# First batch's q and k loaded in rows of eight tokens and transposed by TensorE, and w1 and w2 in chunks of another shape

## The chip, the cores and the metric

The kernel runs on one core of a Trainium2 chip. It is one launch. The time is device microseconds of that core, and the number that is compared is the median of the runs. The engines are TensorE (PE in the profile, its weight loads PEld), VectorE (DVE), ScalarE (ACT), GpSimd (POOL) and SyncE (SP), which issues the DMA transfers. Each engine works through its own instructions strictly in order.

## The reference, cut to what matters

```
B, H, S, D = 8, 8, 576, 64;  pool = 8
k_p = k.reshape(B, H, 72, 8, D).mean(axis=3)          # v_p likewise
scores = q @ k_p.T / sqrt(D)                          # 576 x 72 for each of 64 heads
attn = exp(scores - max);  attn = attn / (attn.sum + 1e-09)
x = (attn @ v_p), heads side by side                  # 4608 tokens x 512
a = x @ w1;  b = x @ w2                               # 512 -> 1024
x = ((a * b) @ w3) @ w_out                            # 1024 -> 1024 -> 512
h = x @ w_in;  g = h / (1 + exp(-1.702 h));  out = g @ w_out2   # 512 -> 2048 -> 512
```

q, k and v are float32, the weights are float64.

## The kernel before

All large products run as three matmuls of values that are split into a rounded part and a remainder (`split`, `mm3`). The float64 weights come in as pairs of 32-bit words and are turned into float32 on the chip. There are three stages.

*The start-up.* `Conv.step` converts one chunk of 128x512 weights in each call: ACT writes two pieces (L166, L167), DVE shifts (L168) and merges (L171), GpSimd adds (L174). The intermediate e lies either in one of two PSUM banks (`acc` in the profile) or in the SBUF tile `cv`. A later call splits the result (L104). A chunk of w3 is transposed on TensorE between (L476). w3 times w_out is multiplied out to one matrix wp (L113 to L115, into `acc`), a product for each chunk that is ready; two rows of wp are open at a time.

Beside it runs the attention of batch 0. A *pair* is two heads of one batch; pairs 0 to 3 are batch 0. A pair passes through steps that `tick` calls in turn: g0 (k and q into the layout that the scores need, sums of k over eight tokens), g1 (scores, L271; their maximum, L276; the subtraction, L278), g2 (exp), g3 (normalize, L292 to L295), g4 (transposed weights), g6 (times v; writes x, L382 and L383). For pairs 0 to 3, g4 lets TensorE transpose; later pairs are transposed by DVE in g3 (L306, tile p). In g0, `g_load` has fetched k and q as four blocks each, with a head's 32 of 64 columns in 32 partitions (`load_blocks`, L228). DVE transposes them in 32x32 blocks (L254 for k, L255 for q) and sums k over eight tokens (L257). ACT puts the sums into the block-diagonal kbd (L259, L260), which is the moving operand of the scores.

*The main loop.* Nine blocks of 512 tokens, eight f each: x·w1 and x·w2 into the banks wk0 and wk1, the product a·b on DVE (L612), and the product of the step before with wp into `acc`. Two ticks of the attention run in each f, so later pairs are computed beside it. The weights w1 and w2 are kept in tiles that are freed in the last block. Some of the freed tiles serve as landing places for the first loads of the next stage: four x tiles (L602) and one of w_in (L606). Which f they start at is set by `FA`.

*The second MoE* (from L692 on).

What sets the order: the calls in the loop over `conv.step` and `tick` give the program order, and a scheduler then sets the order of the instructions on each engine before the run. All DMA transfers stand in one order on SP. An SP issue waits for the eighth issue before it to land, and for its buffer to be free. `take` and `give` hand out the slots (tiles of 128x1024 words), in which chunks, w3 tiles and x lie; a slot is free for the next load when all its readers are done.

## Time and profile before

| | us |
|---|---|
| runs | 1561.65, 1558.10, 1560.19 |
| median | 1560.19 |
| profiled execution | 1560.06 |
| its span | 1558.3 |
| TensorE busy in the span | 1498.2 (96%) |
| DVE busy | 982.5 (63%) |
| ACT busy | 618.4 (40%) |
| GpSimd busy | 586.3 (38%) |
| mean granted clock | 0.974 |

The profiled execution is 1.76 us longer than its span.

How the rows below are read. A row of the table by stretches gives a stretch, its length and then for each engine the busy time and, in brackets, the instructions; PEclk is the granted clock of TensorE as a share of 2.4 GHz; the DMA share is that of the core's 16 DMA engines. A row of the timeline gives the start, the time to the end of the last of the instructions it groups, engine, line, operation, output and input tile, form and count, and in square brackets the idle time before it and what ended it. A row of the grouped instructions gives the form, count, busy time in us and mean ns of one, and after the bar the idle time before them and its releasers. Tile names stand without their numbers there. SPq is the queue of SP; what counts there is the time of issue. A float32 matmul of unsplit values, as L271's, shows two records for each call.

### The profile page before, as it was taken

The page shows a single profiled execution, that of the slowest core. Times are in us where ns is not written, and L with a number is a line of the kernel's source. Part 1 is how long each engine was busy: PE and PEld are TensorE (multiplying, and loading weights), DVE is VectorE, ACT ScalarE, POOL GpSimd, SP SyncE. Part 2 cuts the span into 40 slices and gives each one's busy share as a digit, 9 for nine tenths or more (in the row PEclk, how much of TensorE's full clock was granted, in tenths as well). Part 3 has the DMA queues.
Part 4 walks back from the last instruction along what each step waited for, and adds up shares of the span by engine and source line. Part 5 has one row for each costly group of instructions (what it writes and reads, how often), then busy time and mean ns, then how long its engine had stood idle before and what let it go on. Part 6 is the DMA issues. An engine that isn't in the chain of part 4 may idle for free.

```text
span 1558.3 us, 19571 instructions
## 1 busy us (share of the span) xinstructions
PE 1498.2 (96%) x6728; PEld 1235.8 (79%) x6728; DVE 982.5 (63%) x1810; ACT 618.4 (40%) x1202; POOL 586.3 (38%) x660
## 2 busy tenths in 40 slices
PE   5866999999999999999989999999999999999998
PEld 4744888888888888887868888888888888888887
DVE  8899888787787877569563334463446254734441
ACT  7774443433443434366643323242234222422331
POOL 7688555555555545369462211100110011101110
PEclk9965999999999999999989999999999999999999
DMA  9962223323232320189769343423343233423310
GB/s 289 242 162 53 54 53 67 68 59 68 52 73 47 77 43 35 42 309 371 303 211 391 107 149 115 132 92 117 126 130 114 101 115 122 149 69 127 125 52 28
DMA packets 225444, 196.33 MB, mean 126 GB/s; under 512 B 158784, under 2 KB 175168, under 8 KB 225344
## 3 DMA queue, kind: packets, MB, share of 16 engines
q1 hardware_dynamic: 224768, 194.03, 41.1%
q8 instruction: 53, 0.87, 0.2%
q10 hardware_dynamic: 576, 1.05, 0.2%
q14 instruction: 47, 0.39, 0.1%
HBM read 150.99 MB, written 44.04 MB: 125 GB/s over the span
## 4 chain that ended last, share of the span: by engine, by line
PE 85%; DVE 6%; DMA 3%; issue 2%; ACT 2%; SPq 1%; POOL 0%; DVEq 0%; ACTq 0%; POOLq 0%
PE bk L692 22%; PE bk L113 8%; PE bk L115 8%; PE bk L114 8%; PE wk L114 8%; PE wk L115 8%; PE wk L113 8%; PE acc L113 4%; PE acc L114 4%; PE acc L115 4%; PE wk L271 2%; DMA s<-in_moe_w_dram 2%; DVE cv L171 1%; SPq L228 1%; DVE s L104 1%
## 5 line engine op out<-in xcount | busy, mean ns | idle before, releaser
L692 PE MATMUL bk<-xM,st 128*128 128x512 f32 x1080 | 261.4, 389 | 0.0
L113 PE MATMUL wk<-s,s 128*128 128x512 f32 x576 | 230.9, 403 | 8.8 <-DVE s L104 4.4
L692 PEld LDWEIGHTS bk<-xM,st 128*128 128x128 f32 x1080 | 202.6, 188 | 42.5 <-ACT o L709 0.4
L114 PE MATMUL wk<-s,s 128*128 128x512 f32 x576 | 228.6, 397 | 6.9 <-DVE s L383 6.9
L115 PE MATMUL wk<-s,s 128*128 128x512 f32 x576 | 228.1, 397 | 0.0
L113 PE MATMUL bk<-wo,mv 128*128 128x512 f32 x576 | 224.1, 389 | 0.1
L114 PE MATMUL bk<-wo,mv 128*128 128x512 f32 x576 | 224.1, 389 | 0.0
L115 PE MATMUL bk<-wo,mv 128*128 128x512 f32 x576 | 210.0, 389 | 0.0
L306 DVE STREAM_TRANSPOSE p<-s_t 32x160 f32<-32x160 f32 (+1 forms) x560 | 178.5, 319 | 11.0
L828 POOL TENSOR_TENSOR s<-s,sg 128x512 f32<-128x512 f32 x32 | 41.4, 1292 | 333.2 <-ACT sg L827 333.2
L113 PE MATMUL acc<-s,s 128*128 128x512 f32 x352 | 134.6, 404 | 8.6 <-ACT s L103 8.1
L104 POOL TENSOR_TENSOR s<-a,s 128x512 fp32r<-128x512 f32 x56 | 72.4, 1294 | 186.4 <-ACT s L103 145.9
L114 PE MATMUL acc<-s,s 128*128 128x512 f32 x352 | 141.3, 401 | 0.3 <-POOL s L104 0.3
L115 PE MATMUL acc<-s,s 128*128 128x512 f32 x352 | 140.8, 400 | 0.3 <-DVE s L104 0.3
L113 PEld LDWEIGHTS wk<-s,s 128*128 128x128 f32 x576 | 110.2, 192 | 33.7 <-DVE s L104 6.0
L114 PEld LDWEIGHTS wk<-s,s 128*128 128x128 f32 x576 | 110.5, 192 | 30.6 <-DVE s L383 8.3
L115 PEld LDWEIGHTS wk<-s,s 128*128 128x128 f32 x576 | 110.4, 192 | 23.4
L113 PEld LDWEIGHTS bk<-wo,mv 128*128 128x128 f32 x576 | 108.1, 188 | 23.0 <-ACT mv L103 0.5
L115 PEld LDWEIGHTS bk<-wo,mv 128*128 128x128 f32 x576 | 108.1, 188 | 22.5
L114 PEld LDWEIGHTS bk<-wo,mv 128*128 128x128 f32 x576 | 108.1, 188 | 22.4
L174 POOL TENSOR_TENSOR cv<-cv,s 128x512 int32<-128x512 int32 x72 | 99.7, 1389 | 56.2 <-DVE cv L171 23.9
L844 DVE TENSOR_TENSOR q<-bk,m 128x512 f32<-128x512 f32 x32 | 22.1, 692 | 150.7 <-PE bk L692 150.7
(155 smaller groups left out, 2546.1 us busy)
## 6 DMA issues: line engine op xcount, KB each, us to landing
st<-wind SPq DMA_DIRECT2D x89, 512.0 KB, 3.7
s<-in_moe_w_dram SPq DMA_DIRECT2D x32, 512.0 KB, 6.4
wind<-s SPq DMA_DIRECT2D x32, 512.0 KB, 5.7
s<-in_moe_w_out_dram SPq DMA_DIRECT2D x24, 512.0 KB, 6.6
s<-wind SPq DMA_DIRECT2D x23, 512.0 KB, 3.7
kr<-in_k_dram SPq DMA_DIRECT2D x128, 72.0 KB, 2.5
qr<-in_q_dram SPq DMA_DIRECT2D x128, 72.0 KB, 2.5
out_dram<-o SPq DMA_DIRECT2D x36, 256.0 KB, 2.0
```

The source lines that it names most:

```text
L104: lo_eng.tensor_tensor(out=dst[:, 1], in0=src, in1=f32(dst[:, 0]), op=ALU.subtract)
L113: nc.tensor.matmul(o, a[:, 0, a_sl], b[:, 0, b_sl], start=first, stop=False)
L114: nc.tensor.matmul(o, a[:, 0, a_sl], b[:, 1, b_sl], start=False, stop=False)
L115: nc.tensor.matmul(o, a[:, 1, a_sl], b[:, 0, b_sl], start=False, stop=last)
L171: nc.vector.scalar_tensor_tensor(out=wu, in0=hi_w, scalar=0x80000000, in1=eu, op0=ALU.bitwise_and, op1=ALU.bitwise_or)
L174: nc.gpsimd.tensor_tensor(out=w.bitcast(I32), in0=w.bitcast(I32), in1=lo_w.bitcast(I32), op=ALU.add)
L228: nc.sync.dma_start(dst[32 * c:32 * c + 32], src[b, 2 * hp + c // 2, :, 32 * (c % 2):32 * (c % 2) + 32].rearrange("(g t) d -> t g d", t=32))
L271: nc.tensor.matmul(sc[half][:, i * KW:(i + 1) * KW], qT[:, sl(tt)], mov, start=True, stop=True)
L306: nc.vector.transpose(out=dst[:, :nt, 32 * c:32 * c + 32], in_=s_t[32 * c:32 * c + 32, :nt, 32 * r:32 * r + 32])
L692: nc.tensor.matmul(o, w[:, x, m], b[:, y], start=first and n == 0, stop=last and n == 2, skip_group_check=True)
L828: eng.tensor_tensor(out=v, in0=v, in1=sg, op=ALU.mult)
L844: nc.vector.tensor_tensor(out=q_, in0=o, in1=m1, op=ALU.add)
```

## The change

For the four pairs of batch 0 (`n < NS`), q and k are loaded in rows of eight tokens: a partition holds eight consecutive tokens of a head, 512 numbers, so that 72 partitions hold a head, and one DMA (L242) fetches the two heads of a pair. The tiles come from the slots. `g0_first` takes the place of g0's DVE work. TensorE multiplies pieces of 72x64 with the identity: for k, 16 calls, which accumulate the eight tokens of a row into columns 288 to 359 of the bank wk2, so that the sum over eight tokens comes out of the product (L267); for q, 8 calls for each half of the tokens into wk2 and wk3 (L275). DVE copies the first half into qT and ACT the second (L278).

`g_load` is called two pairs ahead instead of one, pairs 0 and 1 are loaded before most of the weights (depth 2, then 9), ticks start at the third step instead of the fifth, and the loop has two steps more. The chunks of w1 and w2 are 256 rows of w by 256 columns, instead of 512 by 128, and the loop over f picks its half of such a tile; w1's lower parts of the split go to GpSimd and w2's to DVE as before. `FA` is 3 instead of 2, and the tiles are given back two f at a time. In the new file the lines stand lower: L168 is L169, L171 is L172, L254 is L288, L271 is L305, L306 is L340, L383 is L417, L612 is L654, L692 is L734.

```diff
@@ -54,6 +54,7 @@
     NB = NT // T
     NG = B * HP
     NPE = HP
+    NS = HP
     SB = S // 32
     TT = (S + P - 1) // P
     KW = 2 * SK
@@ -148,7 +149,7 @@
                 t = take((P, T, 2), U32)
                 d = t.rearrange("p n two -> p (n two)")
                 nc.sync.dma_start(
-                    d if len(src.shape) == 2 else d.rearrange("p (c m) -> p c m", c=KM), src)
+                    d if len(src.shape) == 2 else d.rearrange("p (c m) -> p c m", c=src.shape[1]), src)
                 self.staged.append((t, turn, done))
 
         def step(self):
@@ -234,6 +235,13 @@
             if n >= NG:
                 return
             b, hp = divmod(n, HP)
+            if n < NS:
+
+                for g, src in ((g_k, k), (g_q, q)):
+                    g[n] = take(dtype=F32)
+                    nc.sync.dma_start(
+                        g[n][:SK], src[b, 2 * hp:2 * hp + 2].rearrange("h (s u) d -> s h (u d)", u=POOL))
+                return
             g_k[n] = pa.tile([P, S], F32, name="kr", tag="raw", bufs=4).rearrange("p (g d) -> p g d", d=32)
             load_blocks(g_k[n], k, b, hp)
             g_q[n] = pa.tile([P, S], F32, name="qr", tag="raw", bufs=4).rearrange("p (g d) -> p g d", d=32)
@@ -248,7 +256,33 @@
             nc.sync.dma_start(g_v[n], vr[:P])
             nc.sync.dma_start(vtr[:KT], vr[P:])
 
+        def g0_first(n):
+
+            kn, qn = g_k.pop(n), g_q.pop(n)
+            ps = wk[2:]
+            w = POOL // 2 * SK
+            kp = ps[0][:, w:w + SK]
+            for a in range(2):
+                for u in range(POOL):
+                    nc.tensor.matmul(kp[sl(a, D)], kn[:SK, a, sl(u, D)], ident[:SK, :SK],
+                                     start=u == 0, stop=u == POOL - 1)
+            nc.scalar.copy(kbd[:D, 0], kp[:D])
+            nc.scalar.copy(kbd[D:, 1], kp[D:])
+            qv = qT[:, :S].rearrange("p (s u) -> p u s", u=POOL)
+            for h, eng in ((0, nc.vector.tensor_copy), (1, nc.scalar.copy)):
+                for i in range(POOL // 2):
+                    for a in range(2):
+                        nc.tensor.matmul(
+                            ps[h][sl(a, D), sl(i, SK)], qn[:SK, a, sl(POOL // 2 * h + i, D)],
+                            ident[:SK, :SK], start=True, stop=True)
+                eng(qv[:, POOL // 2 * h:POOL // 2 * (h + 1)],
+                    ps[h][:, :w].rearrange("p (u s) -> p u s", s=SK))
+            give(kn, qn)
+            g_load(n + 2)
+
         def g0(n):
+            if n < NS:
+                return g0_first(n)
             kr, qr = g_k.pop(n), g_q.pop(n)
             kT = pa.tile([P, S], F32, name="kT", tag="kT")
             nc.vector.transpose(out=kT, in_=kr.rearrange("p g d -> p (g d)"))
@@ -258,7 +292,7 @@
                 out=ks, in_=kT.rearrange("p (s u) -> p s u", u=POOL), op=ALU.add, axis=AX.X)
             nc.scalar.copy(kbd[:D, 0], ks[:D])
             nc.scalar.copy(kbd[D:, 1], ks[D:])
-            g_load(n + 1)
+            g_load(n + 2)
 
         def g1(n):
             sc = (wk[2], wk[3])
@@ -505,7 +539,7 @@
                         w = wp_s[it] = take()
                         split(w, acc[it % 2], nc.vector)
 
-        FA = 2
+        FA = 3
         n_mm, seen, seen_o = {}, [], []
 
 
@@ -524,24 +558,31 @@
         for it in range(2, NIT):
             for jh in range(2):
                 add_3(it, jh)
-        for f in range(NF1):
-            conv.add(col_tile(w1, f), None,
-                     conv.to(w1_s, f, a=f - FA if 0 <= f - FA < NA else None))
-            conv.add(col_tile(w2, f), None, conv.to(w2_s, f, nc.vector))
-
+
+        slots_a = list(range(NA))
+        for h in range(NF1 // 2):
+            for w, w_s, eng in ((w1, w1_s, nc.gpsimd), (w2, w2_s, nc.vector)):
+                for c in range(KM // 2):
+                    conv.add(w[sl(c, 2 * P), sl(h, 4 * P)].rearrange("(c p) m -> p c m", p=P), None,
+                             conv.to(w_s, (c, h), eng, a=slots_a.pop(0) if h and slots_a else None))
+
+        conv.depth = 2
         conv.load()
         g_load(0)
         v_load(0)
+        g_load(1)
+        conv.depth = 9
+        conv.load()
         conv.ps = acc[2:]
         n3 = 8 + 2 * NIT
         done3 = []
-        for i in range(n3 + 4):
+        for i in range(n3 + 6):
             key = conv.step()
             if done3:
                 w3_mm(done3.pop(0))
             if key is not None:
                 done3.append(key)
-            if i >= 4 and tick_n[0] < 20:
+            if i >= 2 and tick_n[0] < 20:
                 tick()
         conv.depth = 8
         give(*(wo_s.pop(j) for j in list(wo_s)))
@@ -590,12 +631,13 @@
                 if conv.busy():
                     conv.step()
                 pa_, pb_ = wk[0], wk[1]
-                for ps, w in ((pa_, w1_s[f]), (pb_, w2_s[f])):
+                h, j = divmod(f, 2)
+                for ps, w_s in ((pa_, w1_s), (pb_, w2_s)):
                     for c in range(KM):
-                        mm3(ps, w, sl(c), x[c], slice(0, T), c == 0, c == KM - 1)
+                        mm3(ps, w_s[c // 2, h], sl(c % 2 * 2 + j), x[c], slice(0, T), c == 0, c == KM - 1)
                 if blk == NB - 1:
-                    give(w1_s.pop(f))
-                    give(w2_s.pop(f))
+                    if j:
+                        give(*(w_s.pop((c, h)) for w_s in (w1_s, w2_s) for c in range(KM // 2)))
                     if 0 <= f - FA < KM:
 
                         t = take_a(f - FA)
```

The first place is DVE's order around pair 0's q and k. Before:

```order
L171 SCALAR_TENSOR_TENSOR cv_310<-s12_142,acc3_69 128x512
L104 TENSOR_TENSOR s2_266<-cv_201,s2_266 128x512
L168 TENSOR_SCALAR acc2_68<-acc2_68 128x512
L254 STREAM_TRANSPOSE kT_219<-kr_146 128x576
L104 TENSOR_TENSOR s4_348<-cv_260,s4_348 128x512
L171 SCALAR_TENSOR_TENSOR cv_338<-s13_144,acc2_68 128x512
L255 STREAM_TRANSPOSE qT_114<-qr_151 128x576
L257 TENSOR_REDUCE ks_222<-kT_219 128x72
L104 TENSOR_TENSOR s25_386<-wk0_70,s25_386 128x512
L168 TENSOR_SCALAR acc3_69<-acc3_69 128x512
L171 SCALAR_TENSOR_TENSOR cv_380<-s14_165,acc3_69 128x512
L276 TENSOR_REDUCE nm_250<-wk2_72 128x6
```

After:

```order
L169 TENSOR_SCALAR acc3_69<-acc3_69 128x512
L172 SCALAR_TENSOR_TENSOR cv_165<-s6_130,acc3_69 128x512
L105 TENSOR_TENSOR s0_183<-cv_157,s0_183 128x512
L169 TENSOR_SCALAR acc2_68<-acc2_68 128x512
L172 SCALAR_TENSOR_TENSOR cv_173<-s11_143,acc2_68 128x512
L105 TENSOR_TENSOR s23_234<-wk0_70,s23_234 128x512
L278 COPY qT_114<-wk2_72 128x4x72
L169 TENSOR_SCALAR acc3_69<-acc3_69 128x512
L169 TENSOR_SCALAR acc2_68<-acc2_68 128x512
L172 SCALAR_TENSOR_TENSOR cv_228<-s12_145,acc3_69 128x512
L172 SCALAR_TENSOR_TENSOR cv_249<-s13_147,acc2_68 128x512
L310 TENSOR_REDUCE nm_239<-wk2_72 128x6
```

Two transposes and the sum (L254, L255, L257) stood between conversions, with 23 instructions ahead of the first. In their place is one copy, L278, with ten instructions ahead of it; the scores' maximum (L276, now L310) has moved from row 32 to row 16.

The second place is SP's order at the start (vr and vtr are v). Before:

```order
L150 DMA s12_142<-in_moe_w3_dram 128x1024
L150 DMA s13_144<-in_moe_w_out_dram 128x1024
L228 DMA kr_146<-in_k_dram 32x18x32 x4
L228 DMA qr_151<-in_q_dram 32x18x32 x4
L248 DMA vr_156<-in_v_dram 128x512
L249 DMA vtr_120<-in_v_dram 16x512
L150 DMA s14_165<-in_moe_w3_dram 128x1024
L150 DMA s15_173<-in_moe_w_out_dram 128x1024
```

After:

```order
L151 DMA s5_128<-in_moe_w_out_dram 128x1024
L151 DMA s6_130<-in_moe_w3_dram 128x1024
L242 DMA s7_132<-in_k_dram 72x2x512
L242 DMA s8_134<-in_q_dram 72x2x512
L256 DMA vr_136<-in_v_dram 128x512
L257 DMA vtr_120<-in_v_dram 16x512
L242 DMA s9_139<-in_k_dram 72x2x512
L242 DMA s10_141<-in_q_dram 72x2x512
L151 DMA s11_143<-in_moe_w_out_dram 128x1024
L151 DMA s12_145<-in_moe_w3_dram 128x1024
L151 DMA s13_147<-in_moe_w_out_dram 128x1024
```

Nine chunks of weights stood ahead of pair 0's blocks, of which there were eight. Now two chunks stand ahead of it, and pair 1 follows before the third chunk.

The third place is DVE's order up to the first a·b of the main loop (L612, now L654). Before:

```order
L306 STREAM_TRANSPOSE p0_1079<-s_t_118 32x4x32 x2
L306 STREAM_TRANSPOSE p0_1079<-s_t_118 32x5x32 x2
L383 TENSOR_TENSOR s28_1012<-wk3_73,s28_1012 128x64
L306 STREAM_TRANSPOSE p0_1079<-s_t_118 32x4x32 x2
L306 STREAM_TRANSPOSE p1_1080<-s_t_118 32x5x32 x2
L306 STREAM_TRANSPOSE p1_1080<-s_t_118 32x4x32 x2
L276 TENSOR_REDUCE nm_1242<-wk2_72 128x6
L612 TENSOR_TENSOR a_1229<-wk1_71,a_1229 128x512
L276 TENSOR_REDUCE nm_1242<-wk3_73 128x4
L255 STREAM_TRANSPOSE qT_114<-qr_1043 128x576
L278 TENSOR_TENSOR s_t_118<-wk2_72,nm_1242 128x3x144
```

After:

```order
L105 TENSOR_TENSOR s20_1597<-cv_1514,s20_1597 128x512
L329 TENSOR_TENSOR s_t_118<-s_t_118,nm_1004 128x5x144
L417 TENSOR_TENSOR s17_1057<-wk3_73,s17_1057 128x64
L310 TENSOR_REDUCE nm_1366<-wk2_72 128x6
...
L340 STREAM_TRANSPOSE p0_1124<-s_t_118 32x4x32 x2
L340 STREAM_TRANSPOSE p1_1125<-s_t_118 32x5x32 x2
L340 STREAM_TRANSPOSE p1_1125<-s_t_118 32x4x32 x2
L654 TENSOR_TENSOR a_1353<-wk1_71,a_1353 128x512
L310 TENSOR_REDUCE nm_1366<-wk3_73 128x4
L289 STREAM_TRANSPOSE qT_114<-qr_883 128x576
```

L383 of pair 3 (now L417) stood among pair 4's transposes of p (L306, now L340); these now follow it. The first a·b stands in row 200 of the order before and in row 188 now.

## Rows read from the trace of the kernel before

**Rows 1.** Busy time of each engine by stretches of the program (table by stretches).

```profile
0.00:10.00 10.00, 0.51 (x3) 0.52 (x4) 5.00 (x10) 6.38 (x10) 5.01 (x15) 1.00 0.78 281
10.00:50.00 40.00, 32.09 (x125) 23.07 (x124) 37.05 (x60) 32.39 (x64) 31.04 (x33) 0.91 0.98 266
50.00:100.00 50.00, 42.76 (x205) 33.34 (x204) 43.58 (x64) 37.22 (x77) 38.87 (x45) 0.93 1.00 254
100.00:150.00 50.00, 28.42 (x84) 19.22 (x85) 48.82 (x77) 23.13 (x52) 41.72 (x47) 0.50 0.26 52
150.00:200.00 50.00, 50.00 (x231) 41.95 (x230) 44.76 (x105) 21.70 (x48) 29.35 (x41) 0.96 0.28 54
200.00:600.00 400.00, 400.00 (x1929) 338.43 (x1928) 321.21 (x781) 157.82 (x354) 209.31 (x298) 1.00 0.28 59
```

**Rows 2.** Timeline of DVE and TensorE where the main loop starts, 148 to 151 us.

```profile
147.99 0.22 DVE L383 TENSOR_TENSOR s<-wk,s 128x64 fp32r<-128x64 f32 x1
...
150.74 0.69 DVE L612 TENSOR_TENSOR a<-wk,a 128x512 f32<-128x512 f32 x1
...
148.27 1.33 PE L271 MATMUL wk<-kbd,qT 128*128 128x144 f32 x4 [1.63 <-DVE s L383]
```

**Rows 3.** DVE's instructions by line and form, 0 to 150 us.

```profile
L168 DVE TENSOR_SCALAR acc<-acc 128x512 uint32<-128x512 uint32 x28 | 19.3, 690 | 6.0 <-ACT acc L166 5.9
L171 DVE SCALAR_TENSOR_TENSOR cv<-s,acc 128x512 uint32<-128x512 uint32 x28 | 18.8, 675 | 0.5
L171 DVE SCALAR_TENSOR_TENSOR cv<-s,cv 128x512 uint32<-128x512 uint32 x12 | 17.3, 1440 | 0.2
L168 DVE TENSOR_SCALAR cv<-cv 128x512 uint32<-128x512 uint32 x12 | 12.1, 1008 | 2.2 <-ACT cv L166 2.2
L104 DVE TENSOR_TENSOR s<-wk,s 128x512 fp32r<-128x512 f32 x16 | 10.8, 681 | 4.5 <-ACT s L103 4.5
...
L104 DVE TENSOR_TENSOR s<-cv,s 128x512 fp32r<-128x512 f32 x9 | 9.0, 1001 | 0.0
L254 DVE STREAM_TRANSPOSE kT<-kr 128x576 f32<-128x576 f32 x8 | 6.2, 770 | 0.3 <-issue 0.3
...
L257 DVE TENSOR_REDUCE ks<-kT 128x72 f32<-128x576 f32 x7 | 5.1, 731 | 0.0
L255 DVE STREAM_TRANSPOSE qT<-qr 128x576 f32<-128x576 f32 x6 | 4.6, 766 | 0.0
...
L306 DVE STREAM_TRANSPOSE p<-s_t 32x160 f32<-32x160 f32 x10 | 3.3, 334 | 0.1
L306 DVE STREAM_TRANSPOSE p<-s_t 32x128 f32<-32x128 f32 x10 | 3.0, 303 | 0.2
...
L278 DVE TENSOR_TENSOR s_t<-wk,nm 128x432 f32<-128x432 f32 x5 | 2.9, 577 | 0.0
L278 DVE TENSOR_TENSOR s_t<-wk,nm 128x288 f32<-128x288 f32 x5 | 2.3, 451 | 0.1
...
L383 DVE TENSOR_TENSOR s<-wk,s 128x64 fp32r<-128x64 f32 x4 | 0.9, 213 | 0.0
```

**Rows 4.** Timeline of TensorE, scores of pairs 0 and 4.

```profile
24.95 1.49 PE L271 MATMUL wk<-kbd,qT 128*128 128x144 f32 x10
...
133.27 2.77 PE L271 MATMUL wk<-kbd,qT 128*128 128x144 f32 x10 [0.23 <-ACT p L351]
```

**Rows 5.** Timeline of SP's queue, first blocks of k.

```profile
5.91 7.15 SPq L228 DMA_DIRECT2D kr<-in_k_dram  x4
```

**Rows 6.** Table by stretches, 4 to 16 us.

```profile
4.00:16.00 12.00, 4.81 (x14) 3.26 (x14) 10.10 (x16) 10.83 (x19) 8.65 (x7) 1.00 1.05 358
```

**Rows 7.** Timeline of SP and TensorE, end of the main loop.

```profile
781.79 0.38 SPq L606 DMA_DIRECT2D s<-wind  x1
...
812.18 2.88 PE L692 MATMUL bk<-s,s 128*128 128x512 f32 x12
```

## The prediction

> **What bounds the kernel now.** I read the table by stretches first, because a mean over the span says little about a program of three stages [rows 1]. TensorE is busy without a gap from 150 us on (50.00 of 50 us, then 400.00 of 400), at the full clock of 2.4 GHz but for a moment. Before that it has 0.51 + 32.09 + 42.76 + 28.42 = 103.8 us of work in 150 us, so 46.2 us of idle time. The change touches what stands ahead of 150 us, and it is worth what it brings the start of the main loop forward.
>
> In the same 150 us VectorE (DVE) is busy 5.00 + 37.05 + 43.58 + 48.82 = 134.5 us; in the last 50 us it rests for 1.2 us. So I read the timeline at the mark next [rows 2]: TensorE waits 1.63 us for the last L383 (the low half of x for pair 3, done at 148.2), runs four scores and then goes on with x·w1 without a break; the first product a·b on DVE (L612) starts at 150.74. DVE is the bound of the start-up, and what counts is the work that stands ahead of L612 in its order. The other engines have room: ACT is busy 23.13 and GpSimd 41.72 of the last 50 us, and the DMA share there is 0.26. In 10 to 100 us the DMA queues are full (0.98, 1.00), yet DVE is still busy 37.05 of 40 and 43.58 of 50 us.
>
> **The change part by part.** All durations are the means of DVE's groups up to 150 us [rows 3]; the counts are the instructions that stand ahead of the first a·b in the two orders.
>
> Taken away for batch 0's pairs: 4 transposes of k (0.770), 4 of q (0.766), 4 sums over eight tokens (0.731): 4 × 2.267 = 9.07 us. Added: 4 copies of a 128x288 PSUM bank into qT. The trace has no such copy; the nearest row is the subtraction that reads 128x288 from PSUM, 0.451 us. Its bounds are the 64-column L383 (0.213) and the 432-column L278 (0.577). I take 0.451: 4 × 0.451 = 1.80 us (0.85 to 2.31).
>
> Conversions: ahead of the mark, 30 now go through a PSUM bank instead of 28, and those that go through the SBUF tile cv fall from 12 to 9 (L168) and to 7 (L171). A conversion costs DVE 0.690 + 0.675 = 1.365 us by PSUM and 1.008 + 1.440 = 2.448 by cv. The sum is 2 × 1.365 − 3 × 1.008 − 5 × 1.440 = −7.49 us. Of it, 2 × (2.448 − 1.365) = 2.17 us is saved for good; the other 5.3 us moves behind the mark. There DVE has 5.24 us free in 150 to 200 us and 79 us in the next 400 [rows 1], beside a TensorE that never stops; I cost it at nothing. Without that cover it would return whole, 5.3 us.
>
> So DVE has −9.07 + 1.80 − 7.49 = −14.76 us ahead of its first a·b.
>
> Against it stands a wait that was not there. The new copy is DVE's eleventh instruction; behind it are nearly all conversions, so whoever needs w_out and w3 waits with it. Ahead of it stand two short memsets and 3 × (0.690 + 0.675) + 1.001 + 0.681 = 5.8 us of work (three conversions, and an L104 from cv and one from wk). When can it run? Two chunks of 524 KB, then k and q of 295 KB each, 1.64 MB, take 5.8 us at the 281 GB/s of the first 10 us [rows 1]; with the first issue at 0.8 that is 6.6 us. Then TensorE must finish 16 calls for k and 8 for half of q. A call of fp32 is two records: L271 makes 5 calls a pair and shows x10. No row has a 64x72 result. The nearest is L271, 128x144, one record every 0.149 us at the full clock (1.49 us for 10) and every 0.277 at half (2.77 for 10) [rows 4]; half of these, if the time goes with the columns, is 0.075 and 0.139. For 48 records that is 3.6 to 13.3 us, so the copy can start between 10.2 and 19.9 us. Before, DVE had done 5.0 us of work by 10 us and then 0.926 us in each us, so some 5.2 to 14.2 us by then. The loss against the 5.8 us is thus nothing to 8.4 us; I take the middle, 15.1 us, where DVE had done 9.7: 3.9 us lost. The same wait for pairs 1 to 3 I cost at nothing, since their q and k are loaded earlier and their passes stand ahead of their scores; with no cover it is up to 3.9 us for each.
>
> TensorE gets 4 × 32 calls, 256 records: 19 to 71 us by the two bounds, in 46.2 us of idle time. I take 0.11 us, between the two halves: 28 us, covered. Here a rule bears on the sum. In rows, TensorE was busy 28.42 of 50 us at a granted clock of 0.50, thus 1.2 GHz, and 50 of 50 at 0.96 [rows 1]. The Trainium skill, "TensorE: Matmul & The Clock Gate", Part 1: The HAM clock gate, says that the throttled state is the default and that activity releases it; the rows agree. By that rule the added passes help to lift the clock and the cheap price holds; if the passes stay broken up, the dear one does.
>
> DMA: eight block loads a pair become two; the first were issued from 5.91 us on, four in 7.15 us [rows 5], and now stand in places 3 and 4 of SP's order. Pairs 0 and 1 come ahead of most of w_out, which delays a chunk by 0.59 MB, 1.6 us at the 358 GB/s of 4 to 16 us [rows 6]; I count it in the bounds of the start. Another rule speaks against these loads. "DMA: Bandwidth & Descriptors" in the Trainium skill, section "Why a DMA increments its semaphore by 16 and not by 1", lets a transfer use the largest number of engines up to 16 that divides its slowest dimension: 12 for 72 rows. By it, eight loads would take a third longer, estimated 8 × 0.27 = 2.2 us in a full queue, and the sum below would be 1551. No run so far shows a transfer of 72 rows.
>
> Chunks of w1 and w2 of 128x2x512 for 128x4x256 (as many, of as many bytes, in rows twice as long): nothing, as DVE is the later one. With FA = 3 the last loads of the main loop come one f later, about (812 − 150) / 72 = 9.2 us. The load was issued at 781.79 and its first reader ran at 812.18 [rows 7], so 30 us of cover shrink to some 21: nothing. If that cover went, the price would be what exceeds 21 us.
>
> Sum: −14.8 + 3.9 = −10.9 us on the profiled time of 1560.06, thus 1549.2; the profiled time lies 0.13 under the median of 1560.19. I say 1549.
>
> **The rivals.**
> *More is gained.* The mark is the last L383 and not a·b, and the start loses nothing. Ahead of that L383, two more L168 through cv (2 × 1.008) and 14 transposes of p for pair 4 (8 × 0.334 + 6 × 0.303 = 4.5) move behind it [rows 3], so DVE has 21.3 us less: 1560.06 − 21.3 = 1539. For it: TensorE waits for L383 in the trace [rows 2]. Against it: x of pair 3 passes through ACT, GpSimd and TensorE too, and these have not become shorter.
>
> *TensorE's passes eat the gain.* At each of pairs 1 to 3 the copy waits as at the first: 3 × 3.9 = 11.7 us, which is 0.8 more than was won: 1560.9. For it: DVE works strictly in order and the passes of a pair stand among w3's products, which now run later. Against it: 46 us of idle time.
>
> *Slower: TensorE at 1.2 GHz becomes the bound of the start.* The passes are pieces of 72 columns that end in waits; if the engine stays at the lower level, and a 72-column record costs near to a 144-column one, the start is set by TensorE. It decides from 46.2 / 256 = 0.18 us a record. Half way between 0.18 and 0.277, at 0.229, it needs 58.6 us, 12.4 more than there are: 1572; at 0.277 24.7 more: 1585. For it: 0.50 of the clock in 100 to 150 us [rows 1]. Against it: the columns are half of L271's.
>
> **How the numbers follow.** My forecast gets 0.50 with its own range of 1544 to 1555 (the start's loss of 0 to 8.4 us, and what the copies' bounds give); more gained 0.15; gain eaten 0.17; slower 0.18. Of the third case, 0.03 still falls on the faster side, where one of the waits is covered. A measurement of this kernel can tell about 0.2%, 3.1 us, from none: faster 0.68, within 0.2% 0.14, slower 0.18. For the range I go down to 1538 and up to 1570, which leaves out about a tenth at the top and little below.
>
> **What would show it.** Right: a·b's first on DVE at about 140 us and everything behind it the same 11 us earlier; first copy into qT at about 15 us, with idle time in front of it that is released by TensorE; records of the passes at 0.07 to 0.14 us; the stretch from the mark to the first L692 unchanged (661 us). Wrong: DVE idle in front of each of the four copies (third case), TensorE busy without gaps ahead of pair 3's copies at 0.50 of the clock (slower), or a wait of the first L692 on its loads.

## The result and the profile after

The changed kernel takes 1576.08 us (median of 4 runs, 1574.62 to 1577.26), the kernel before 1560.11 beside it. The ratio is 1.0103, 95% interval 1.0085 to 1.0120: 16 us slower, where 11 us less were forecast. The profiled execution took 1574.62 us with a span of 1572.9.

The table by stretches of the changed kernel answers to [rows 1]; its columns are the same.

```profile
0.00:10.00 10.00, 1.73 (x17) 1.76 (x19) 4.34 (x7) 4.31 (x6) 4.48 (x14) 1.00 0.80 222
10.00:50.00 40.00, 31.69 (x223) 23.20 (x220) 32.72 (x55) 31.85 (x63) 31.85 (x35) 1.00 0.93 278
50.00:100.00 50.00, 43.18 (x269) 33.58 (x270) 31.99 (x54) 32.22 (x68) 31.05 (x43) 0.76 0.78 210
100.00:150.00 50.00, 36.97 (x163) 28.51 (x161) 42.97 (x58) 29.60 (x63) 35.78 (x34) 0.81 0.38 93
150.00:200.00 50.00, 42.66 (x183) 34.99 (x184) 48.15 (x100) 18.41 (x41) 33.64 (x41) 0.89 0.21 42
200.00:600.00 400.00, 399.66 (x1925) 337.51 (x1924) 325.53 (x791) 159.89 (x361) 211.72 (x302) 1.00 0.28 61
```

DVE is busy 4.34 + 32.72 + 31.99 + 42.97 = 112.0 us of the first 150, 22 us less than before. The work did go, and none of it came back as time: DVE now stands idle for 38 us instead of 15.5. TensorE no longer works without a gap from 150 us on; it idles 7.3 us in the next 50.

The timeline of DVE at two places of the changed kernel, the first copy into qT and the start of the main loop, answers to [rows 2].

```profile
15.81 0.70 DVE L169 TENSOR_SCALAR acc<-acc 128x512 uint32<-128x512 uint32 x1 [5.34 <-ACT acc L167]
...
17.75 0.68 DVE L278 COPY qT<-wk 128x288 f32<-128x288 f32 x1
...
153.00 0.21 DVE L417 TENSOR_TENSOR s<-wk,s 128x64 fp32r<-128x64 f32 x1
...
154.88 6.65 DVE L340 STREAM_TRANSPOSE p<-s_t 32x160 f32<-32x160 f32 x20
161.56 0.69 DVE L654 TENSOR_TENSOR a<-wk,a 128x512 f32<-128x512 f32 x1
```

The last x of pair 3 is 5 us later than before (153.00, was 147.99), the first a·b 10.8 us (161.56, was 150.74), since all of pair 4's 20 transposes now stand between, where only six stood before:

```profile
148.25 1.97 DVE L306 STREAM_TRANSPOSE p<-s_t 32x128 f32<-32x128 f32 x6
```

The pairs ahead of pair 3 are not late. The last rows of x in DVE's order for pair 2, before and then after:

```profile
131.23 0.21 DVE L383 TENSOR_TENSOR s<-wk,s 128x64 fp32r<-128x64 f32 x1
```

```profile
118.49 0.46 DVE L417 TENSOR_TENSOR s<-wk,s 128x288 fp32r<-128x288 f32 x1 [0.84 <-ACT s L416]
```

Pair 2 is 12.5 us ahead of where it was, pairs 0 and 1 are 11.7 and 19.6 us ahead. Pair 3's scores still begin 15 us earlier (98.5, was 113.7); it loses its lead between these and its x. The same columns for the whole way to the first a·b, and for the part from 120 us on, before and then after:

```profile
0.00:150.74 150.74, 104.53 (x416) 76.69 (x417) 135.16 (x210) 99.54 (x201) 117.38 (x137) 0.79 0.73 191
120.00:150.74 30.74, 21.15 (x61) 14.53 (x62) 29.60 (x54) 12.67 (x31) 26.02 (x32) 0.50 0.31 58
```

```profile
0.00:161.56 161.56, 119.36 (x681) 91.55 (x681) 123.27 (x198) 101.30 (x205) 109.16 (x132) 0.84 0.65 178
120.00:161.56 41.56, 22.76 (x80) 16.45 (x78) 40.08 (x59) 19.68 (x42) 31.41 (x32) 0.67 0.18 42
```

Up to its first a·b DVE has 11.9 us less work (123.27 against 135.16) and 22.7 us more idle time (38.3 against 15.6), and the difference of the two is the 10.8 us. The idle time lies ahead of 120 us; from there on DVE rests for 1.5 us of 41.6. What fills that stretch is work that came late: 12 conversions begin (L169) after 100 us and ahead of a·b, 9 before (L168).

What DVE waited for, and ACT, from 0 to 180 us (columns: us in total, times, longest), before:

```profile
ACT s L167 <- DMA s<-in_moe_w_dram: 14.9, 13, 2.4
...
DVE acc L168 <- ACT acc L166: 5.9, 4, 3.8
...
DVE s L104 <- ACT s L103: 4.7, 5, 2.2
```

After:

```profile
DVE acc L169 <- ACT acc L167: 16.5, 8, 5.3
DVE s L105 <- ACT s L104: 13.6, 9, 4.2
...
ACT s L168 <- DMA s<-in_moe_w_dram: 18.6, 18, 3.3
```

DVE's waits for ACT have grown by 19.5 us. ACT, in its order, waits for chunks that have not come (the name, without its number, stands for w1, w2 and w3), but only 3.7 us more than before. The last chunks, of w1 and w2, do come late: 34 of 40 are issued by 100 us, 40 before. SP's queue shows why; first its timeline, then what ended its waits from 90 to 108 us.

```profile
91.74 16.10 SPq L151 DMA_DIRECT2D s<-in_moe_w_dram  x4
...
123.63 0.38 SPq L151 DMA_DIRECT2D s<-in_moe_w_dram  x1
```

```profile
SPq L151 <- POOL cv L175: 10.9, 2, 8.5
SPq L151 <- PE acc L116: 3.4, 1, 3.4
SPq L151 <- PE wk L275: 3.2, 1, 3.2
```

Four loads take 16 us, for they wait for slots: of conversions not yet done, of w3's tiles whose products TensorE has not done, and of q of pair 3, which the passes read. TensorE's timeline has the passes of pairs 2 and 3, the last product of w3 and the first matmul of the second MoE (812.18 before [rows 7]):

```profile
49.97 2.02 PE L267 MATMUL wk<-ident,s 72*64 72x72 f32 x32 [0.97 <-DVE s L417]
...
85.81 3.68 PE L267 MATMUL wk<-ident,s 72*64 72x72 f32 x32 [1.14 <-DVE s L417]
...
122.06 0.39 PE L116 MATMUL acc<-s,s 128*128 128x512 f32 x1
...
825.62 2.88 PE L734 MATMUL bk<-s,s 128*128 128x512 f32 x12
```

The passes of pair 2 start when L417 has read the banks for x of pair 0, those of pair 3 when it has done so for pair 1. From the first a·b to L734 there are 664.1 us, before 661.4, and behind L734 the two are within 1.2 us. So 13.4 us of the difference lie ahead of L734, and nearly all of these in the start and in the gaps of the first 50 us of the main loop.

### The profile page after: what moved, and what is told of

It reads as the page before. It is cut to its first block, busy times and chain, and to the rows that moved or that the text cites. A ratio compares the mean times of both kernels' runs of the same rounds, so it can differ in the third digit from the quotient of the medians.

```text
span 1572.9 us, 20023 instructions
## 1 busy us (share of the span) xinstructions
PE 1510.9 (96%) x6984; PEld 1247.3 (79%) x6984; DVE 979.3 (62%) x1802; ACT 619.5 (39%) x1206; POOL 587.9 (37%) x660
## 4 chain that ended last, share of the span: by engine, by line
PE 83%; DVE 8%; DMA 2%; issue 1%; POOL 1%; SPq 1%; ACT 1%; DVEq 0%; POOLq 0%; ACTq 0%
PE bk L734 21%; PE bk L114 8%; PE bk L116 8%; PE bk L115 8%; PE wk L114 7%; PE wk L115 7%; PE wk L116 7%; PE acc L114 4%; PE acc L115 4%; PE acc L116 4%; PE wk L305 2%; DVE cv L172 1%; DVE p L340 1%; DVE cv L169 1%; DVE s L105 1%
## 5 line engine op out<-in xcount | busy, mean ns | idle before, releaser
L734 PE MATMUL bk<-xM,st 128*128 128x512 f32 x1080 | 261.4, 389 | 0.0
L734 PEld LDWEIGHTS bk<-xM,st 128*128 128x128 f32 x1080 | 202.6, 188 | 42.5 <-ACT o L751 0.4
L340 DVE STREAM_TRANSPOSE p<-s_t 32x160 f32<-32x160 f32 (+1 forms) x560 | 178.5, 319 | 11.3 <-POOL vt L368 0.5
```

Source lines behind the costliest of these rows:

```text
L340: nc.vector.transpose(out=dst[:, :nt, 32 * c:32 * c + 32], in_=s_t[32 * c:32 * c + 32, :nt, 32 * r:32 * r + 32])
L734: nc.tensor.matmul(o, w[:, x, m], b[:, y], start=first and n == 0, stop=last and n == 2, skip_group_check=True)
```

## The experiments

Ratios are to the kernel before in the same runs, with 95% intervals. A thousandth is 1.56 us. "Chunks" are the loads of the four weights issued by 50 and by 100 us (40 in all), counted from the issue lines; "x" is the start of pair 3's last L383 (L417 and others), "a·b" that of the first. The blocks of edits show the lines that matter and leave out the rest.

| run | ratio | interval | chunks 50 / 100 | x | a·b |
|---|---|---|---|---|---|
| before | | | 26 / 40 | 148.0 | 150.7 |
| changed | 1.0103 | 1.0085 to 1.0120 | 22 / 34 | 153.0 | 161.6 |
| e1_pe_only | 1.0066 | 1.0051 to 1.0081 | 24 / 35 | 147.6 | 155.7 |
| e2_chunks_only | 1.0045 | 1.0030 to 1.0060 | 25 / 39 | 147.1 | 156.2 |
| e3_late_blocks | 1.0104 | 1.0087 to 1.0121 | 22 / 34 | 154.0 | 162.6 |
| e4_old_start | 1.0078 | 1.0060 to 1.0095 | 24 / 36 | 150.3 | 158.2 |
| e5_kq_raw | 1.0043 | 1.0027 to 1.0060 | 31 / 40 | 146.2 | 155.3 |
| e6_k_eighth | 1.0096 | 1.0074 to 1.0118 | 24 / 35 | 149.6 | 153.7 |
| e7_wk01 | 1.0031 | 1.0018 to 1.0044 | 24 / 34 | 130.4 | 137.3 |
| e8_two_steps | 0.9998 | 0.9989 to 1.0007 | 25 / 40 | 153.1 | 153.7 |
| e9_no_transposes | 0.9988 | 0.9978 to 0.9997 | 26 / 40 | 144.8 | 148.1 |
| e10_four_slots | 1.0014 | 1.0004 to 1.0024 | 22 / 39 | 150.1 | 152.2 |
| e11_chunks_by_turns | 1.0031 | 1.0020 to 1.0042 | 25 / 40 | 149.8 | 154.3 |
| e12_tick_19 | 1.0028 | 1.0018 to 1.0039 | 24 / 40 | 148.7 | 151.4 |
| e13_half_slots | 1.0037 | 1.0023 to 1.0051 | 27 / 36 | 145.3 | 149.5 |
| e14_half_slots_early | 1.0018 | 1.0009 to 1.0027 | 27 / 37 | 146.2 | 151.1 |
| e15_g0_before_g6 | 0.9986 | 0.9977 to 0.9996 | 29 / 40 | 139.7 | 148.7 |
| e16_after_tick_5 | 0.9994 | 0.9985 to 1.0003 | 20 / 39 | 138.9 | 147.0 |
| e17_after_g0_first | 1.0002 | 0.9993 to 1.0011 | 21 / 39 | 139.4 | 149.1 |
| e18_after_g0_first_tick_5 | 1.0050 | 1.0037 to 1.0064 | 22 / 39 | 150.2 | 158.5 |

**Which part costs?** e1 is the kernel before with `g0_first` and the loads of L242; e2 is the kernel before with the new chunks, their use in the loop over f, `FA` = 3 and the two steps more; e4 has both with the old start; e3 is the changed kernel with another depth of the loads from pair 4 on.

```diff
# e1, against the kernel before
+            if n < NS:
+                return g0_first(n)
# e2, against the kernel before
-            conv.add(col_tile(w1, f), None,
+                    conv.add(w[sl(c, 2 * P), sl(h, 4 * P)].rearrange("(c p) m -> p c m", p=P), None,
-        FA = 2
+        FA = 3
# e3, against the changed kernel: in g0, for pairs from 4 on
-            g_load(n + 2)
+            g_load(n + 1)
# e4, against the changed kernel; the first two lines in g0 and g0_first
-            g_load(n + 2)
+            g_load(n + 1)
-        conv.depth = 2
-        g_load(1)
-            if i >= 2 and tick_n[0] < 20:
+            if i >= 4 and tick_n[0] < 20:
```

*e1_pe_only*, expected:

> Only the first batch's q and k by TensorE (rows of eight tokens); chunks of w1 and w2, FA, the order of the first loads, the loads one pair ahead and the start of the ticks as before. Theory Q (the loss is SP's queue: earlier and more loads of q, k and v stand ahead of the chunks of w1 and w2): about 1550, 10 us under before. Rival P (TensorE's passes and the waits at the copies cost the time): 1565 to 1576. Rival C (the new chunks of w1 and w2 cost it): about 1550.

*e2_chunks_only*, expected:

> Only the new chunks of w1 and w2, with FA = 3 and the loop two steps longer, which these chunks need, since four of them must be converted before the first f instead of two. Theory Q: 1558 to 1563, no change. Rival P: the same, no change. Rival C: 1568 to 1576, most of the loss.

*e3_late_blocks*, expected:

> The changed kernel, but pairs from 4 on are loaded one pair ahead, as before, and not two; pairs 0 to 3 stay two ahead. Theory Q: a part of the loss comes back, 1563 to 1572, and the last chunk of w2 is issued before 115 us instead of at 123.6. Rivals P and C: 1574 to 1578.

*e4_old_start*, expected:

> TensorE's passes and the new chunks both, but the start as before: weights first, then pair 0, each pair loaded one ahead, ticks from the fifth step. Theory Q: 1550 to 1560, the chunks of w1 and w2 issued by 100 us. Rival P: 1570 to 1576. Rival C: 1568 to 1576.

Theory Q fell: e3 brought nothing. TensorE's passes alone cost 10 us, the chunks alone 7, both with the old start 12 and with the new one 16. e1 and e4 lie in rival P's ranges, e2 between the ranges that were named for it. The parts don't add up, a first sign that it is the order and not a sum of work.

**Is it DVE at all?** *e9_no_transposes* takes the work off DVE and puts it nowhere.

```diff
+            if n < NPE:
+                nc.vector.transpose(out=qT[:, :32], in_=qr[:, 0])
+                nc.vector.tensor_copy(ks, kr.rearrange("p g d -> p (g d)")[:, :SK])
```

> The kernel before, but for pairs 0 to 3 DVE transposes only the first 32 columns of q and copies 72 columns in place of k's transpose and sum (this leaves out the layout that the scores need). DVE has 8 to 9 us less ahead of the main loop, and no engine has more. The step of the prediction that DVE's work sets the start: 1550 to 1553. Rival L (the start is set by chains of waits through all engines in order, and freed DVE time becomes idle time): 1557 to 1562.

DVE's groups of e9 up to 148 us, and then the last x of pair 3 and the first a·b in its timeline:

```profile
L104 DVE TENSOR_TENSOR s<-cv,s 128x512 fp32r<-128x512 f32 x9 | 13.2, 1466 | 0.0
...
L258 DVE COPY ks<-kr 128x72 f32<-128x72 f32 x4 | 3.0, 761 | 0.3 <-DMA kr<-in_k_dram 0.3
...
L257 DVE STREAM_TRANSPOSE qT<-qr 128x32 f32<-128x32 f32 x4 | 0.8, 197 | 0.0
```

```profile
144.76 0.23 DVE L388 TENSOR_TENSOR s<-wk,s 128x64 fp32r<-128x64 f32 x1
...
148.05 0.68 DVE L617 TENSOR_TENSOR a<-wk,a 128x512 f32<-128x512 f32 x1
```

9.07 us went and 3.8 came in their place (the copies took 0.761 us each, not the 0.1 I had thought of), and the memset of qT is 0.5 longer, so the edit takes 4.8 us off DVE. The time fell by 0.0012 x 1560 = 1.9 us (0.5 to 3.4), as rival L had it, and the first a·b came 2.7 us earlier. Up to there DVE was busy 129.5 us instead of 135.2 and idle 18.6 instead of 15.6: more than half of what was freed became idle time. Its terms are not fixed prices either. The L104 from cv took 1466 ns instead of 1001 [rows 3], 4.2 us more over nine, and L168 on cv took 701 instead of 1008, 3.7 us less over twelve. So DVE's sum alone is not what sets the start.

**Is it the passes' own time, the slots, or their place?**

*e5_kq_raw*, expected:

> The kernel with TensorE's passes alone, but q and k of batch 0 in the four buffers of the old block loads (one a head) instead of in slots, so that weights and w3's tiles have all slots as before. Theory S (slots: q's and k's tiles keep the chunks of w1 and w2 from being loaded): 1556 to 1562, last chunk issued by 105 us instead of 118 to 122. Theory B (the passes stand in TensorE's order and wait there for the banks of the pair before, with w3's products behind them, which end at 119 us instead of 91): 1567 to 1572, w3's products still end after 110 us.

*e6_k_eighth*, expected:

> The kernel with TensorE's passes alone, but of k only the first of eight tokens is multiplied (this leaves out seven eighths of k's sum): 28 records less for a pair, 1.8 to 3.2 us of TensorE, 7 to 13 us for four pairs; all waits stay. If the passes' own time is the loss: 1558 to 1563. Theories S and B: 1566 to 1571.

*e7_wk01*, expected:

> The kernel with TensorE's passes alone, but in the banks wk0 and wk1, which w3's transposes use by turns, instead of wk2 and wk3, which scores and x use. The passes then wait for no x of the pair before. Theory B: 1556 to 1563, w3's products end by 105 us. Theory S: 1568 to 1572.

*e10_four_slots*, expected:

> The kernel before, with four of its slots held until the main loop, as many as q and k of two pairs take. Theory S (slots that q and k hold delay the chunks of w1 and w2): 1564 to 1570, last chunk issued after 105 us instead of at 97.6. If slots are not short: 1558 to 1562.

```diff
# e5
-                    g[n] = take(dtype=F32)
+                        t = pa.tile([P, S], F32, name="kq", tag="raw", bufs=4)
# e6
-                for u in range(POOL):
+                for u in range(1):
# e7
-            ps = wk[2:]
+            ps = [wk[(turn_n[0] + i) % 2] for i in range(2)]
# e10
+        hold4 = [take(dtype=F32) for _ in range(4)]
```

The passes' own time is not the loss: with 28 of 64 records of a pair less, e6 was not faster than e1. e5 had its chunks early (31 by 50 us) and won 3.6 us over e1, less than half of what theory S asked for; its ten runs lie far apart, from 1563.4 to 1572.7 us. Something else came late there, as two of the rows of SP's waits from 40 to 130 us show:

```profile
SPq L229 <- PE wk L270: 24.4, 1, 24.4
SPq L151 <- POOL cv L175: 12.4, 4, 7.5
```

The first row is pair 4's blocks, which wait for the passes of pair 3. With four buffers, one pair is in flight, and pair after pair waits for the passes of the one ahead. e10 shows that four slots less cost the old kernel 2.2 us (0.6 to 3.7). e7 can't be read cleanly: its passes write over a transposed chunk of w3 before that is split (so w3 is wrong in part), which ties the two together; it gained 5.5 us over e1. Its first a·b comes 13 us earlier than in the kernel before, but from there to the second MoE it needs 682.3 us instead of 661.4, so an early a·b by itself is no gain. e5, e6 and e7 lie outside all the ranges that were named for them: neither theory S nor theory B holds as it was put.

e13 keeps two pairs in flight with half of the slots, e14 loads pair 0 early in it, and e15 calls the passes of pairs 1 to 3 ahead of the x of the pair two before (what `g0_first` does behind the passes, the next loads and the return of the slots, moves with them):

```diff
# e13, against e5
+                    if n % 2:
+                        t = take(dtype=F32)
# e14, against e13
+        conv.depth = 2
         conv.load()
         g_load(0)
         v_load(0)
+        conv.depth = 9
+        conv.load()
# e15, against e13
             elif s == 1:
                 if n < NG:
                     g1(n)
+                if n + 1 < NS:
+                    g0(n + 1)
             elif s == 2:
...
-                if n + 1 < NG:
+                if NS <= n + 1 < NG:
                     g0(n + 1)
```

*e13_half_slots*, expected:

> The kernel with TensorE's passes alone; pairs 0 and 2 in the four old buffers (one a head), pairs 1 and 3 in slots, so that two pairs are in flight and at most two slots are held. Theory S with late q and k as the rest of the loss of the kernel that uses the old buffers alone: 1556 to 1563, 40 chunks issued by 100 to 105 us. If slots are not the cause: 1566 to 1572.

*e14_half_slots_early*, expected:

> The same, with pair 0's q, k and v behind two chunks of weights instead of nine, as in the changed kernel. If an early pair 0 helps once the slots are free: 2 to 6 us under the kernel with pairs 1 and 3 in slots. If the start order costs, as it seemed between the changed kernel and the one with the old start: 2 to 4 us over it.

*e15_g0_before_g6*, expected:

> As the kernel with pairs 1 and 3 in slots, but a pair's passes come right behind the scores of the pair before, ahead of that pair's x, so that they no longer wait for its last L417 to free the banks. If these waits (2 us for each of pairs 2 and 3) and what queues behind them on TensorE cost time: 2 to 6 us under it. If not: within 2 us of it.

e13 missed theory S's range: 5.8 us over before. e14 is 3 us under it, as an early pair 0 should be. e15 differs from e13 in the place of this call alone and is 8 us faster, more than the 2 to 6 expected; it is the one kernel with the passes whose interval lies under the kernel before (by 2.2 us, 0.6 to 3.6). Its rows, DVE and TensorE:

```profile
139.70 0.23 DVE L428 TENSOR_TENSOR s<-wk,s 128x64 fp32r<-128x64 f32 x1
142.03 6.65 DVE L351 STREAM_TRANSPOSE p<-s_t 32x160 f32<-32x160 f32 x20
148.71 0.69 DVE L660 TENSOR_TENSOR a<-wk,a 128x512 f32<-128x512 f32 x1
...
90.31 0.40 PE L116 MATMUL acc<-s,s 128*128 128x512 f32 x1
```

w3's products end at 90 us as in the kernel before (91; 113 in e13), x of pair 3 is 8 us earlier than before. e17 does the same to the changed kernel, e16 starts its ticks at the fifth step, e18 does both:

```diff
-            if i >= 2 and tick_n[0] < 20:     # e16, e18
+            if i >= 4 and tick_n[0] < 20:
```

*e16_after_tick_5*, expected:

> The changed kernel with ticks from the fifth step as before; all else, the early loads too, as in the changed kernel. If the early ticks are what the start order costs (about 4 us between the changed kernel and the one with the old start): 1570 to 1573. If the early loads two pairs ahead, which hold slots, are: 1574 to 1577.

*e17_after_g0_first*, expected:

> The changed kernel, with nothing else altered than that the passes of pairs 1 to 3 come right behind the scores of the pair before, ahead of that pair's x. Theory B (the passes stand on TensorE behind waits for the banks of x, and w3's products and with them the chunks behind them): most of the 16 us comes back, 1556 to 1564, w3's products end by 100 us instead of 122, 38 or more chunks issued by 100 us instead of 34. If the early ticks cost for another reason: 1570 to 1577.

*e18_after_g0_first_tick_5*, expected:

> The same with ticks from the fifth step: both remedies together. If both remove the same wait: 1555 to 1561, as either alone at its best. If they add up: 1548 to 1555, under the kernel before and the changed one.

e17 gives back the whole 16 us by moving one call. Its passes of pair 2, the matmul that waits ahead of the main loop with what ACT waits for ahead of it, and its last x and first a·b:

```profile
42.53 2.02 PE L267 MATMUL wk<-ident,s 72*64 72x72 f32 x32
...
149.01 0.79 PE L114 MATMUL wk<-s,s 128*128 128x512 f32 x1 [5.28 <-ACT a L653]
...
147.80 0.67 ACT L394 CAST ph<-p 128x576 fp32r<-128x576 f32 x1 [5.62 <-DVE p L340]
...
139.39 0.21 DVE L417 TENSOR_TENSOR s<-wk,s 128x64 fp32r<-128x64 f32 x1
...
142.47 6.64 DVE L340 STREAM_TRANSPOSE p<-s_t 32x160 f32<-32x160 f32 x20
149.13 0.69 DVE L656 TENSOR_TENSOR a<-wk,a 128x512 f32<-128x512 f32 x1
```

Pair 2's passes run 7 us earlier and wait for nothing; x of pair 3 ends 13.6 us earlier than in the changed kernel. w3's products end at 109 us, not by the 100 that I had expected. e16 gives back as much, which I had not expected (1570 to 1573 at best). In it the passes stay where they are, and TensorE waits longer for the banks ahead of pair 2's than in the changed kernel (0.97):

```profile
51.51 3.68 PE L267 MATMUL wk<-ident,s 72*64 72x72 f32 x32 [4.88 <-DVE s L417]
```

So that wait by itself is not the loss. What e16 and e17 have in common is that 39 chunks are issued by 100 us, that w3's products end at 109 us, that 7 conversions and not 12 begin between 100 us and a·b, and that DVE idles 27.6 and 29.2 us up to a·b instead of 38.3. e18 missed altogether: 7.8 us over before, with 39 chunks as well, but 10 such conversions and 32.6 us of idle time. The move that gains 16 us in e17 against the changed kernel costs 9 us in e18 against e16. So the two remedies are not two waits that add up; each shifts the whole order.

**The chunks, and the end of the start.**

```diff
# e8, against the kernel before
-        for i in range(n3 + 4):
+        for i in range(n3 + 6):
# e11, against e2
-            for w, w_s, eng in ((w1, w1_s, nc.gpsimd), (w2, w2_s, nc.vector)):
-                for c in range(KM // 2):
+            for c in range(KM // 2):
+                for w, w_s, eng in ((w1, w1_s, nc.gpsimd), (w2, w2_s, nc.vector)):
# e12, against the kernel before, in both places
-        while tick_n[0] < 20:
+        while tick_n[0] < 19:
```

*e8_two_steps*, expected:

> The kernel before, with the loop of the start two steps longer, as the new chunks of w1 and w2 need it, and nothing else. If the two more conversions ahead of the main loop cost the 6.5 us of the chunks: 1564 to 1568. If the shape of the chunks or FA costs them: 1558 to 1562.

*e11_chunks_by_turns*, expected:

> The new chunks of w1 and w2 alone, loaded by turns (w1, w2, w1, w2) instead of two of w1 and then two of w2. If the order of the chunks, with two splits of w2 on DVE in a row, costs the 6 us: 1558 to 1562. If it is that the first f waits for four chunks, or the scheduler's other order: 1564 to 1569.

*e12_tick_19*, expected:

> The kernel before, with one tick less ahead of the main loop, so that pair 4's 20 transposes of p (6.6 us of DVE) come behind the first a·b. If DVE's order at the end of the start sets the main loop's start: 1553 to 1557. If the last x of pair 3 alone sets it: 1558 to 1562.

e8 (`n3 + 6` in the kernel before) changes nothing. e11 (the loops over c and over w1 and w2 exchanged) may win back 2 us of e2's 7, within the intervals. So it is neither the two conversions nor, for the most part, the order of the chunks; FA is no cause in the traces either, with 662.0 us from a·b to the second MoE in e2 and 661.4 before. What the shape costs stays open. e12 (`tick_n[0] < 19`) did not do what it was meant to. In its trace all 20 transposes of pair 4 still stand ahead of the first a·b:

```profile
143.97 4.66 DVE L306 STREAM_TRANSPOSE p<-s_t 32x160 f32<-32x160 f32 x14
...
148.91 1.96 DVE L306 STREAM_TRANSPOSE p<-s_t 32x128 f32<-32x128 f32 x6
...
151.40 0.69 DVE L612 TENSOR_TENSOR a<-wk,a 128x512 f32<-128x512 f32 x1
```

So it says nothing on its question. It was 4.4 us slower, outside both ranges, and this stayed unexplained.

## Why the prediction was wrong

*The step that failed* is the second of the first part: DVE is the bound of the start-up, and "what counts is the work that stands ahead of L612 in its order". DVE's 134.5 busy us of 150 were read as a bound, and its waits were taken to stay as they were but for 3.9 us. The work fell by 11.9 us up to the first a·b, not far from the 14.76 of the sum. But DVE's idle time up to there rose by 22.7 us, 19.5 of them waits for ACT, and a·b came 10.8 us later. e9 shows the same without any new work: 5.7 us less to do up to a·b, 3.0 us more idle time, 1.9 us won in all. At the very end DVE does set the pace, with 1.5 us of rest from 120 us to a·b; what was freed ahead of that could not be used, since the conversions that fill the end came late.

That the order makes them late, and not the work, is shown by e16 and e17, which do the same work in another order and have the 16 us back. By which wait it does so stays open. Before, k and q were transposed by DVE without a bank, at any time after they had landed; now they take wk2 and wk3 behind x. The chain that suggests itself, x of a pair frees the banks, the next passes run, the copies, the scores, and so on to the next x, is not borne out: TensorE's own idle time for these banks is 2.1 us (0.97 and 1.14), x of pairs 0 to 2 comes earlier than before, and e16 has its time back with a longer wait there. A way through the slots, in which w3's products end late and hold slots that the last chunks need, fits the changed kernel, e1, e3, e4 and e6 (products to 116 us or later, 34 to 36 chunks by 100 us). It does not fit e18, which has 39 chunks by then, nor e5, which has all 40, and both are slow.

*The sum's terms.* The conversions and transposes did go, as counted. The copy took 0.68 us at its first, against 0.451 taken and 0.577 as upper bound. The start loss was near by luck: the copy came at 17.75 instead of 15.1, within 10.2 to 19.9, but the passes that it needs were done by 13 us, and what DVE had waited for was a chunk (5.34 us, L167). The records of the passes came at 0.063 us (k, 2.02 for 32) at the full clock and 0.115 at half (3.68), those of q at 0.045 and 0.077: inside the bounds of 0.075 and 0.139 or under. (The prediction names 0.139 as the upper price, but its 13.3 us for 48 records and its 71 us for 256 take 0.277.) Pair 0's took 0.113 (3.29 for 29), near the price at half, although the row of that stretch gives 1.00; the trace has no record of the clock ahead of 21.3 us. By TensorE's time the term was right, "covered"; by its order it was not.

*The cover that was not there.* "The same wait for pairs 1 to 3 I cost at nothing, since their q and k are loaded earlier and their passes stand ahead of their scores": loaded they were, but the passes needed banks, which the prediction did not follow. The wait itself is small, 2.1 us for pairs 2 and 3 and nothing for pair 1. The prediction had it as a rival, at up to 3.9 us a pair, and dated it from the data and not from the banks.

*The rivals.* The slower one had the sign and not the mechanism: TensorE still idled 36.4 us in the first 150, where the rival needs none, and e6, with fewer records, was no faster. The granted clock fell to 0.76 in 50 to 100 us (0.93 before) and rose to 0.81 in 100 to 150 (0.50), at 43.18 and 36.97 us of work. The rule that the Trainium skill gives in "TensorE: Matmul & The Clock Gate", Part 1, that activity releases the throttle, agrees with the second stretch; in the first the level fell though the engine did as much as before (42.76).

*The loads.* With nearly the same DMA share (0.80, before 0.78) the first 10 us moved 222 GB/s instead of 281, and the passes began at 8.27 and not at 6.6. The trace's semaphores show these loads at work: k of pair 0, issued at 1.7 us, has twelve landing steps between 7.15 and 8.13 us, a chunk of 128 rows has sixteen. Of the chunk issued at 4.8 us, behind the loads of q and k, four steps come at 10.0 to 10.5 us and the other twelve at 14.5 to 15.1, and this is the chunk that ACT and through it DVE wait for in the 5.34 us. That agrees with the rule that the Trainium skill has in "DMA: Bandwidth & Descriptors", "Why a DMA increments its semaphore by 16 and not by 1", by which a transfer uses the largest number of engines up to 16 that divides its slowest dimension, twelve for 72 rows. The prediction left its price, an estimated 2.2 us, out of the sum; the chunk's last twelve steps came some 4.5 us behind its first four.

*Right:* FA's 9 us were covered (664.1 us from a·b to L734, against 661.4, with 7.3 us of gaps in the first 50).

## What to carry to other kernels

An engine at 90% busy is not yet the bound: take the work off it and look whether the end moves, before pricing what replaces it. Count its idle time as a term of its own: here the work fell about as forecast and the idle time grew by twice as much. When work goes to another engine, follow its buffers too: here DVE needed no PSUM bank and TensorE did. And where a scheduler and in-order queues set the order, the place of a step can be worth more than its duration, and has no fixed price either: one call moved was worth 16 us in e17 and cost 9 us in e18, while 28 records less for each pair gained nothing.

## What was not expected

Two remedies that each gave back the 16 us cost 7.8 us together (e18). In e15 to e17 the last x of pair 3 comes 8 to 9 us earlier than in the kernel before, and the whole is no more than some 2 us faster: pair 4's 20 transposes, 6.6 us, stand in DVE's order ahead of a·b; ACT waits for them 5.62 us in e17, and TensorE, behind ACT, 5.28. To get them behind the first a·b would be the next thing to try; it was not run, and e12 shows that one tick less does not by itself do it. In e7 they do stand behind it (a·b at 137.3), and the main loop lost more than was won.
